# Row tiles that take every fourth row: a GeGLU feed-forward kernel on one Trainium2 core

## The chip, the cores and the metric

The kernel runs on one core of one Trainium2 chip. The metric is device time in microseconds (us) of one execution. "Median" is that of several executions. One execution of each kernel also left a profile, and this is the trace that is read. The span in a profile is about 1.9 us shorter than the device time of the same execution (before: 540.66 us and 538.8 us).

## The reference

```python
B, S, Dm, Df = 1, 2048, 1024, 3584          # all arrays bf16
def reference(x, w_gate, w_up, w_down):
    g = einsum("bsd,df->bsf", x, w_gate)
    u = einsum("bsd,df->bsf", x, w_up)
    h = gelu_tanh(g) * u
    return einsum("bsf,fd->bsd", h, w_down)
```

## The kernel before

The kernel makes the two products with fewer multiplications by block sums (the tiles `t`, `s`, `q`) and keeps TensorE (PE) busy nearly all the time. It works in two passes of 1024 rows. Only the first 512 rows of x come in as plain row tiles, which PE transposes; later rows come through transposing DMAs. All DMAs are issued by SyncE (SP), in program order, so the weights of the first matmuls stand in the queue behind the four x tiles. The first 8 us or so, until the row of matmuls that is never broken again, are called the head below. A load "lands" when its last bytes are reported in place.

```python
P, N = 128, 512;  NS = N // P                # 4 row tiles in 512 rows; Dm = 1024, so a row of x is 2 KB

def load_x(c):                               # called once, with c = 0
    t = []
    for i in range(NS):
        xn = slot([P, Dm], bf16, "xn")
        r0 = c * N + i * P
        nc.sync.dma_start(out=xn, in_=x2[r0 : r0 + P, :])
        t.append(xn)
    return t

def turn(xT, xn, c, i):                      # 8 transposes on PE, then copies to xT
    ...
        nc.tensor.transpose(tp[:, ko, :], xn[i][:, ko * P : (ko + 1) * P], ident)
    ...

xT = new_x()
xn0 = load_x(0)
wf = wpool.tile([P, 2, NKB, 2 * P], bf16, name="w")
for k0, k1 in ((0, 2), (2, 5), (5, NKB)):    # six slices of the first weights, pieces of 512 B
    load_wf(nc.sync, k0, k1)
w = load_w(1)
for ko in range(NKB):
    transposing(xT, 1, ko, N)                # rows 512 to 1023
...
keep_warm(NWARM, N)                          # matmuls of a constant while x comes in
for i in range(NS):
    if i == 2:
        keep_warm(2, 2 * P)
    turn(xT, xn0, 0, i)
plain(bank[0:4], 0, range(0, 2), parts=2)    # the first real matmuls: xT against wf
...

def store(ip, c, i, dc, put):                # 128 rows x 512 columns of the output
    st = slot([P, N], bf16, "st")
    put(st)
    r0 = (2 * ip + c) * N + i * P
    nc.sync.dma_start(out=out2[r0 : r0 + P, dc * N : (dc + 1) * N], in_=st)
```

## Time and profile before

| | before |
|---|---|
| median of the first three runs | 539.89 us (539.87 to 540.21) |
| span of the profiled run | 538.8 us |
| PE busy | 534.1 us, 99% |
| first unbroken row of matmuls starts at | 7.91 us |
| fourth x tile: issue, landing | 2.12 us, 6.99 us |

These are lines of the page of the kernel before: its span, busy time by engine (busy us, share, instructions), and the chain that ended last by engine.

```profile
span 538.8 us, 7447 instructions
...
PE 534.1 (99%) x2409; PEld 381.2 (71%) x2409; DVE 341.5 (63%) x524; ACT 261.4 (49%) x463; POOL 238.5 (44%) x215
...
PE 98%; DMA 1%; SPq 0%; ACT 0%; issue 0%
```

PE is the limit, and there is next to nothing else in the chain. This is the chain that ended last, in order of time (start, length in us, what), of the kernel before:

```profile
2.12 4.87 DMA xn<-in_x_dram
6.99 0.05 issue
7.04 0.62 PE bank L447 x8
7.66 0.22 PE bank L111 x2
7.88 0.03 issue
7.91 527.77 PE bank L111 x2366
```

The chain starts with the wait for the last x tile, goes through its eight transposes, and then stays on PE without a break for 527.77 us.

The timeline of PE in the first microseconds, before (start, us, engine, line, operation; in brackets the idle time ahead of the group and what ended it):

```profile
3.71 1.71 PE L447 MATMUL bank<-ident,xn 128*128 128x128 bf16 x16
...
6.31 1.35 PE L447 MATMUL bank<-ident,xn 128*128 128x128 bf16 x16 [0.66 <-DMA xn<-in_x_dram]
7.49 1.68 PE L111 MATMUL bank<-xT,w 128*128 128x256 bf16 x12
```

And the tiles `xn` before: their issue, and the time from issue to landing over the four of them.

```profile
L440 SPq DMA_DIRECT2D xn<-in_x_dram x4: 392/420/432, 0.7 to 2.1; - x4
...
DMA to landing us min/median/max: 2.8/3.8/4.9
```

The first tile lands 2.8 us after its issue, the fourth 4.9 us after. What the DMA moved meanwhile is in the table by windows (last three columns: granted PE clock, DMA share, GB/s):

```profile
2.50:5.00 2.50, 2.50 (x17) 1.62 (x16) 0.19 (x1) 0.00 (x0) 0.00 (x0) 1.00 1.04 316
5.00:7.50 2.50, 1.73 (x25) 1.28 (x24) 1.04 (x2) 2.02 (x2) 0.00 (x0) 1.00 1.11 320
```

### The profile page before, as it was taken

The numbers are of one execution on the slowest core, as the hardware profiler recorded it, in microseconds if no ns is written. First come the engines' busy times: TensorE is split into PE (matmuls) and PEld (weight loads), VectorE is DVE, ScalarE is ACT, GpSimd is POOL, SyncE is SP. The second block draws the span as 40 slices with busy tenths as digits, with TensorE's granted clock in tenths as the row PEclk, the third lists the DMA queues.
The fourth block names the chain that finished last, engine by engine and source line by source line (L and its number), as shares of the span: only waits on it lengthen the run. The fifth ranks groups of instructions, "written<-read, shape, count | busy, mean of one in ns | idle before, by whom it ended". The sixth has DMA issues, their size and how long they took to land.

```text
span 538.8 us, 7447 instructions
## 1 busy us (share of the span) xinstructions
PE 534.1 (99%) x2409; PEld 381.2 (71%) x2409; DVE 341.5 (63%) x524; ACT 261.4 (49%) x463; POOL 238.5 (44%) x215
## 2 busy tenths in 40 slices
PE   8999999999999999999999999999999999999997
PEld 5568686867677746888867677676868685488886
DVE  2986766767676894694955455555554649676730
ACT  2556675766666410255355555555555551114431
POOL 1179966677773500000097767676766600000000
DMA  9675656749472999989872223242420049573751
GB/s 243 157 185 168 185 176 175 220 133 260 131 235 72 381 366 297 307 192 296 238 195 80 78 80 88 70 118 63 133 71 9 2 147 390 184 236 96 237 181 51
DMA packets 108198, 93.29 MB, mean 173 GB/s; under 512 B 17280, under 2 KB 93056, under 8 KB 108160
## 3 DMA queue, kind: packets, MB, share of 16 engines
q1 hardware_dynamic: 108160, 92.82, 59.4%
q8 instruction: 19, 0.31, 0.3%
q14 instruction: 19, 0.16, 0.1%
HBM read 74.45 MB, written 15.20 MB: 166 GB/s over the span
## 4 chain that ended last, share of the span: by engine, by line
PE 98%; DMA 1%; SPq 0%; ACT 0%; issue 0%
PE bank L111 98%; DMA xn<-in_x_dram 1%; SPq L440 0%; PE bank L447 0%; ACT st L412 0%
## 5 line engine op out<-in xcount | busy, mean ns | idle before, releaser
L93 POOL TENSOR_TENSOR s<-w 128x512 fp32r<-128x512 bf16 x102 | 119.2, 1189 | 163.2 <-DVE t L90 86.0
L111 PE MATMUL bank<-t,s 128*128 128x512 f32 x648 | 151.7, 390 | 0.0
L111 PEld LDWEIGHTS bank<-t,s 128*128 128x128 f32 x648 | 121.6, 188 | 25.5
L111 PE MATMUL bank<-xT,w 128*128 128x512 bf16 (+1 forms) x504 | 109.7, 376 | 0.0
L107 ACT COPY p<-bank 128x512 f32<-128x512 f32 x124 | 69.9, 590 | 45.4 <-PE bank L111 44.9
L111 PEld LDWEIGHTS <-w 128*128 128x128 bf16 x504 | 48.1, 98 | 58.1 <-issue 3.4
L90 DVE TENSOR_TENSOR hT<-g,bank 128x512 bf16<-128x512 f32 x112 | 76.8, 687 | 17.5 <-PE bank L111 4.5
L90 DVE TENSOR_TENSOR sum<-bank,p 128x512 f32<-128x512 f32 x54 | 37.3, 691 | 79.5 <-PE bank L111 78.4
L179 ACT ACTIVATE g<-sum 128x512 f32<-128x512 f32 x81 | 51.4, 635 | 74.5 <-DVE sum L90 74.2
L111 PE MATMUL bank<-q 128*128 128x512 f32 x240 | 58.9, 389 | 0.0
L93 POOL TENSOR_TENSOR s<-w,s 128x512 fp32r<-128x512 bf16 x50 | 57.7, 1176 | 0.0
L93 POOL TENSOR_TENSOR s<-s,w 128x512 fp32r<-128x512 f32 x50 | 57.2, 1165 | 0.0
L111 PE MATMUL bank<-t,sa 128*128 128x512 f32 x216 | 55.9, 401 | 0.0
L111 PE MATMUL bank<-tb,s 128*128 128x512 f32 x216 | 53.3, 389 | 0.0
L107 ACT COPY u<-bank 128x512 f32<-128x512 f32 x62 | 35.5, 589 | 33.5 <-PE bank L111 33.2
L111 PEld LDWEIGHTS bank<-q 128*128 128x128 f32 x240 | 45.0, 188 | 9.4
L111 PE MATMUL bank<-raw,hT 128*128 128x512 bf16 x224 | 48.7, 379 | 0.0
L102 ACT CAST tb<-raw 128x512 fp32r<-128x512 bf16 x28 | 17.3, 626 | 62.1 <-PE bank L111 27.6
L111 PEld LDWEIGHTS bank<-t,sa 128*128 128x128 f32 x216 | 40.6, 188 | 9.5
L111 PEld LDWEIGHTS bank<-tb,s 128*128 128x128 f32 x216 | 40.5, 188 | 8.4
L90 DVE TENSOR_TENSOR bank<-bank,p 128x512 f32<-128x512 f32 x54 | 37.7, 699 | 8.8 <-PE bank L111 6.2
L90 DVE TENSOR_TENSOR q<-hT 128x512 fp32r<-128x512 bf16 x56 | 38.4, 685 | 4.3 <-PE bank L111 4.3
(44 smaller groups left out, 442.1 us busy)
## 6 DMA issues: line engine op xcount, KB each, us to landing
raw<-in_w_down_dram SPq DMA_DIRECT2D x76, 256.0 KB, 5.0
q<-td SPq DMA_DIRECT2D x60, 256.0 KB, 5.1
w<-in_w_gate_dram SPq DMA_DIRECT2D x27, 512.0 KB, 5.9
w<-in_w_up_dram SPq DMA_DIRECT2D x27, 512.0 KB, 7.0
td<-m SPq DMA_DIRECT2D x12, 768.0 KB, 4.5
w<-td SPq DMA_DIRECT2D x6, 1024.0 KB, 10.0
out_dram<-st SPq DMA_DIRECT2D x32, 128.0 KB, 1.7
td<-w SPq DMA_DIRECT2D x2, 768.0 KB, 6.2
```

The costliest lines, as they stand in the source:

```text
L90: nc.vector.tensor_tensor(out=out, in0=a, in1=b, op=op)
L93: nc.gpsimd.tensor_tensor(out=out, in0=a, in1=b, op=op)
L102: nc.scalar.copy(out=t, in_=src)
L107: nc.scalar.copy(out=t, in_=ps)
L111: nc.tensor.matmul(ps, lhsT=lhs, rhs=rhs, start=start, stop=stop, skip_group_check=True)
L179: nc.scalar.activation(g, src, ACT.Gelu_apprx_tanh)
```

## The change

The four row tiles of the first 512 rows are dealt out differently: tile i takes rows i, i+4, i+8 and so on. Each tile is still 128 pieces of 2 KB, but they start 8 KB apart (this distance is called the pitch below), and a tile spans 1 MB of memory and not 256 KB. The matmuls see the same rows in another order. The outputs of those rows come out in that order too, so their eight stores (of 32) write to every fourth row. The change gives no reason; a different layout in memory, of these reads and of eight stores, is all that it can act on.

```diff
 def store(ip, c, i, dc, put):
     ...
-    r0 = (2 * ip + c) * N + i * P
-    nc.sync.dma_start(out=out2[r0 : r0 + P, dc * N : (dc + 1) * N], in_=st)
+    r0 = (2 * ip + c) * N
+    rows = slice(i, N, NS) if ip == c == 0 else slice(r0 + i * P, r0 + i * P + P)
+    nc.sync.dma_start(out=out2[rows, dc * N : (dc + 1) * N], in_=st)

 def load_x(c):
     ...
-        r0 = c * N + i * P
-        nc.sync.dma_start(out=xn, in_=x2[r0 : r0 + P, :])
+        nc.sync.dma_start(out=xn, in_=x2[c * N + i : (c + 1) * N : NS, :])
```

No engine gains or loses an instruction, and their order stays the same on every engine.

## The prediction

> **What bounds the kernel.** TensorE. The page's first table gives PE 534.1 us of a 538.8 us span (99%); the chain of waits is 98% matmuls of one line, unbroken from 7.91 to 535.7 us. The part of the chain that is not PE is the head: 4.87 us in which the fourth x tile is awaited (issued at 2.12 us, landed at 6.99), then eight transposes, then the first matmuls, which wait another 0.31 us for the first w_up slice. By the timeline PE idles about 1.6 us from its first warm-up matmul to 8 us, so little more can be won there.
>
> **What the change does.** Four loads of 256 KB (x, first 512 rows) and eight of the 32 stores (128 KB each) keep their count, bytes and pieces: 128 rows of 2 KB in, 128 rows of 1 KB out. Only the pitch in HBM changes, from 2 KB to 8 KB between row starts, so each tile spans the whole first 1 MB instead of a quarter. Every engine's instructions stand in the same order. The transposed columns hold other rows, and the stores undo it. No compute is removed or added.
>
> **Cost.**
> - Loads. In the first 8 us the DMA moves 310 to 370 GB/s in most half-microsecond windows, so the head is limited by x (1 MB, an estimate of 3 us at that rate) and the weights queued behind it. The tiles land 2.8, about 3, 4.6 and 4.9 us after issue; the third is late beside one straggling packet of 1.5 us (median 84 ns). The pitch may move stragglers by a fraction of a microsecond. A check for pitch: q from the td scratch, 256 KB in 2 KB rows at 84 KB pitch, lands in 5.1 us median, w_down tiles of 256 KB in 5.0 us. So I expect no slower rate. The Trainium skill (DMA: Bandwidth & Descriptors, Latency and other measured facts, "HBM row pitch at large powers of two") tabulates row pitches from 512 KiB up, slower from 2 MiB on; 8 KiB is far below, and no run here yet shows it. Effect: 0, give or take 0.7 us, one for one in the total.
> - Stores. Their landing (1.7 us median) is awaited once by DVE (1.1 us, at 264 us, for a buffer of the t sums); those sums are done by 273 us and PE takes them at 279 us. Even a doubled landing stays off the chain. Effect: 0.
>
> **Prediction.** 539.8 us, 8 in 10 between 538.7 and 541.0. Chance of faster by over 2%: 0.005; within 2%: 0.985; slower by over 2%: 0.01.
>
> **Right or wrong in the profile.** Right: PE busy 534 us within 0.5, the chain still 98% matmuls, x loads landing in 2.8 to 5 us, the unbroken matmuls starting within 0.7 us of before, stores landing in 1.7 to 2.5 us, DVE's wait for a store under 3 us. Any change of the total equals the shift of that start (7.91 us before). Wrong: x landing after 8 us, or a new PE gap later.
>
> **What would make it wrong.** A pitch of 8 KB that piles the engines' reads onto fewer parts of HBM: x would land at half rate and the head lose an estimated 3 us, still 0.6%. Or reads of one contiguous 256 KB are the ones that collide (the straggler), and spreading them brings the head forward by up to 1.3 us. Or a late store holds a buffer that PE needs soon: a new gap near 215 or 265 us.

## The result, and the profile after

| | before | after |
|---|---|---|
| median, 6 runs each | 540.01 us (539.84 to 540.21) | 541.78 us (541.11 to 542.14) |
| ratio | | 1.0031 (95%: 1.0018 to 1.0044) |
| span of the profiled run | 538.8 us | 540.1 us |
| unbroken matmuls start at | 7.91 us | 9.02 us |

Ratios here and below are the mean time of one kernel's runs over that of the other's runs of the same rounds, so they are not quite the ratio of the medians quoted. The change costs 1.8 us here, 0.3%: well under 2%, but clear of the spread. The whole range of after lies above 541.0 us, the top of the predicted range.

The page after:

```profile
span 540.1 us, 7447 instructions
...
PE 534.6 (99%) x2409; PEld 381.0 (71%) x2409; DVE 341.5 (63%) x524; ACT 261.2 (48%) x463; POOL 237.8 (44%) x215
...
PE 98%; DMA 1%; SPq 0%; ACT 0%; issue 0%
```

The chain that ended last, after:

```profile
2.12 5.93 DMA xn<-in_x_dram
8.05 0.05 issue
8.10 0.62 PE bank L447 x8
8.72 0.25 PE bank L111 x2
8.97 0.05 issue
9.02 527.96 PE bank L111 x2366
```

The work is the same. The fourth x tile takes 5.93 us and not 4.87 us, and the unbroken matmuls start 1.11 us later. That is most of the 1.3 us between the two spans; the row of matmuls itself took 0.19 us more in this trace. The timeline of PE after shows new gaps, each ended by an x tile:

```profile
4.23 1.78 PE L447 MATMUL bank<-ident,xn 128*128 128x128 bf16 x16 [0.31 <-DMA xn<-in_x_dram]
...
6.57 0.62 PE L447 MATMUL bank<-ident,xn 128*128 128x128 bf16 x8 [0.34 <-DMA xn<-in_x_dram]
8.10 0.62 PE L447 MATMUL bank<-ident,xn 128*128 128x128 bf16 x8 [0.91 <-DMA xn<-in_x_dram]
8.58 0.39 PE L111 MATMUL bank<-xT,w 128*128 128x256 bf16 x2
```

All x tiles land later, while their issues take as long as before:

```profile
L440 SPq DMA_DIRECT2D xn<-in_x_dram x4: 392/418/432, 0.7 to 2.1; - x4
...
DMA to landing us min/median/max: 3.4/4.4/5.9
```

The windows after show the same loss as a rate: the same queue of loads moves 238 and 262 GB/s in place of 316 and 320. The DMA share (time of packets over the time of 16 engines; it passes 1 where packets overlap) falls with it, from 1.04 and 1.11 to 0.77 and 0.95. By the packet records the median x packet took 84 ns in both traces. So most of the loss is time with fewer packets under way, and not slower packets.

```profile
2.50:5.00 2.50, 2.19 (x12) 1.00 (x10) 0.00 (x0) 0.00 (x0) 0.00 (x0) 1.00 0.77 238
5.00:7.50 2.50, 1.85 (x21) 1.17 (x18) 0.97 (x2) 1.44 (x2) 0.00 (x0) 1.00 0.95 262
```

The first weight slices moved with x: they landed 4.8 us after their issue before, and 5.9 us after it now. The Trainium skill ("DMA: Bandwidth & Descriptors", "Queues, rings and completion order") says that each DMA engine consumes its descriptors in ring order. The landings agree with that: what stands behind x slips by the same 1.1 us.

What opens the unbroken row is a load of weights into PE (PEld), and it waits for the first slice of `w_up`, the second load behind x. First before, then after (timeline of PEld, window 2:10):

```profile
7.91 2.07 PEld L111 LDWEIGHTS <-w 128*128 128x128 bf16 x18 [0.31 <-DMA w<-in_w_up_dram]
...
9.01 0.99 PEld L111 LDWEIGHTS <-w 128*128 128x128 bf16 x10 [0.32 <-DMA w<-in_w_up_dram]
```

That slice landed at 7.87 us before and at 8.97 us after. In all eleven kernel traces with four x tiles and these slices behind them (before, after, e1, e2, e6 to e10, f2, f3) this weight load starts 0.04 to 0.05 us after that landing. So the chain's first step, the wait for x, is not quite the last wait: x and the slice behind it slip together, and the slice releases the row.

### The profile page after: what moved, and what is told of

The parts are those of the page before. It is cut to its first block, busy times and chain, and to the rows that moved or that the text cites. A ratio compares the mean times of both kernels' runs of the same rounds, so it can differ in the third digit from the quotient of the medians.

```text
span 540.1 us, 7447 instructions
## 1 busy us (share of the span) xinstructions
PE 534.6 (99%) x2409; PEld 381.0 (71%) x2409; DVE 341.5 (63%) x524; ACT 261.2 (48%) x463; POOL 237.8 (44%) x215
## 4 chain that ended last, share of the span: by engine, by line
PE 98%; DMA 1%; SPq 0%; ACT 0%; issue 0%
PE bank L111 98%; DMA xn<-in_x_dram 1%; SPq L440 0%; PE bank L447 0%; ACT st L413 0%
```

## The experiments

**Theory H**: the loss is in the head. At a pitch of 8 KB the x loads run slower, and PE's first matmuls wait for them and for the weights behind them. **Rival S**: the eight stores are slower, and hold buffers that something needs. **Rival N**: the one trace of each is luck. (The trace before has a straggler, an x packet of 1.5 us where the median is 84 ns; it is not a lucky trace.)

Inside H it was open whether any break of the sequence is slow, or a pitch that is a power of two, or 8 KB alone, and whether other traffic has a part in it.

The table gathers what ran as a whole kernel. "Before" is the kernel before in the same rounds; each of the four batches of rounds (e1 and e2; e6 to e8; e9 to e12; f2 and f3) ran on another chip. Landing is that of the fourth x tile after its issue, in the one trace of each.

| run | what | median | before | ratio (95%) | landing |
|---|---|---|---|---|---|
| e1 | strided loads alone | 541.34 us | 540.26 us | 1.0018 (1.0005 to 1.0030) | 5.2 us |
| e2 | strided stores alone | 540.27 us | 540.26 us | 0.9997 (0.9983 to 1.0010) | 4.2 us |
| e8 | the change again | 541.29 us | 540.22 us | 1.0023 (1.0009 to 1.0037) | 5.4 us |
| e6 | every second row | 540.42 us | 540.22 us | 1.0006 (0.9994 to 1.0019) | 5.0 us |
| f2 | every third row | 540.33 us | 540.19 us | 1.0003 (0.9991 to 1.0016) | 4.4 us |
| f3 | every eighth row | 540.33 us | 540.19 us | 1.0008 (0.9994 to 1.0022) | 4.3 us |
| e7 | rows dealt, 32 apart | 540.66 us | 540.22 us | 1.0012 (1.0000 to 1.0025) | 4.3 us |
| e9 | weights held back, rows as before | 543.48 us | 540.26 us | 1.0061 (1.0049 to 1.0074) | 4.2 us |
| e10 | weights held back, every fourth row | 544.63 us | 540.26 us | 1.0084 (1.0070 to 1.0098) | 4.4 us |
| e11 | pieces of 4 KB | 540.84 us | 540.26 us | 1.0022 (1.0008 to 1.0035) | |
| e12 | one load, pieces of 8 KB | 542.56 us | 540.26 us | 1.0040 (1.0026 to 1.0053) | |

### e1 and e2: one half of the change each

```diff
 e1: load_x as after, store as before      (output wrong on purpose: its rows are permuted)
 e2: load_x as before, store as after      (likewise)
```

> The first 512 rows are loaded with the new pitch, but their outputs are stored in sequence as before, so the output is wrong on purpose. Theory H (the loss sits in the head: the four x loads run slower at a pitch of 8 KB): the whole loss appears, 1.3 to 2.2 us over before, with the fourth x tile landing about 5.5 to 6.2 us after its issue. Rival S (the stores, or the buffers they hold, cost it): within 0.4 us of before.

> The loads are as before and only the eight stores go to every fourth row, so the output is wrong on purpose. Theory H: within 0.3 us of before. Rival S: 1.3 to 2.2 us over before.

The loads alone cost 1.1 us, the stores alone nothing. The chains that ended last say where, first of e1 and then of e2:

```profile
3.07 5.39 DMA w<-in_w_up_dram
8.46 0.05 issue
8.51 527.75 PE bank L111 x2366
```

```profile
2.12 4.17 DMA xn<-in_x_dram
6.29 0.05 issue
6.34 0.62 PE bank L448 x8
6.96 0.38 PE bank L111 x2
7.33 0.03 issue
7.37 527.76 PE bank L111 x2366
```

The rows of matmuls are equally long (527.75 and 527.76 us), and start 1.14 us apart. In e1 the chain's head is the first `w_up` slice and not x: the slice that releases the row in e2 too. Rival S falls. The loss in e1 (1.1 us) is at the low end of what was expected or under it (1.3 to 2.2 us), and its fourth tile landed at 5.2 us, not 5.5 to 6.2. The repeat, e8, gives the same 1.1 us for the whole change; the 1.8 us of the first rounds was not met again.

> The changed kernel itself, timed on the same chip as the others. Theory H: 1.0 to 1.9 us over before, the first unbroken matmuls later by the same amount as in the earlier trace, about 1.1 us or more.

In e8's trace the unbroken matmuls start at 8.54 us. Against the first trace before (7.91 us) that is only 0.63 us later, less than the 1.1 us expected; against e2's, whose loads are the same as before (7.37 us), it is 1.17 us. The trace before has the straggler, so e2's is the better base.

### e3 and e4: the loads by themselves

A kernel with nothing but loads: four x tiles issued one after the other, the next group when all four have landed; twelve groups of each kind, in rotating order.

```diff
+for name, rows in order:                     # row steps 1, 2, 3, 4, 5, 8, 16; in e4 four layouts
+    for i, t in enumerate(tiles):
+        nc.sync.dma_start(out=t, in_=rows(i))
+    for t in reversed(tiles):                # the next group waits for these reads
+        nc.vector.tensor_copy(out=acc[:, 0:64], in_=t[:, 0:64])
```

> Only loads, output wrong on purpose: groups of four 256 KB tiles of x in 2 KB rows, each group started when the one before has landed, twelve times each at row steps 1, 2, 3, 4, 5, 8 and 16 (2 to 32 KB pitch), in rotating order. Time from a group's first issue to its last landing. Theory H: step 4 takes 0.8 to 2 us longer than step 1. Within H: if a power-of-two pitch piles reads on fewer parts of memory, steps 4, 8 and 16 are slow and 3 and 5 as fast as 1, the loss growing with the step; if what counts is that neighbouring rows are no longer read together, steps 2 to 16 are all slow alike. Rival N (not the pitch but the unlucky start of a run): all steps within 0.3 us.

Median landing after issue, twelve groups each, in us:

| row step (pitch) | 1 (2 KB) | 2 (4) | 3 (6) | 4 (8) | 5 (10) | 8 (16) | 16 (32) |
|---|---|---|---|---|---|---|---|
| first tile | 2.6 | 2.6 | 2.6 | 3.2 | 2.7 | 3.0 | 2.7 |
| fourth tile | 4.0 | 3.8 | 4.2 | 4.3 | 4.1 | 3.8 | 3.9 |

(With steps 2 and 3, here and in e5, some of the four tiles read the same rows again, so the steps from 4 on are the cleaner comparison.) Step 4 is the slowest, but by only 0.3 us, at the fourth tile and from a group's first issue to its last landing (5.60 against 5.32 us), which is not the 0.8 to 2 us that theory H expected. The loss does not grow with the pitch. So H has the right place, but loads of x by themselves do not explain 1.1 us.

> Only loads, output wrong on purpose: groups of four tiles as in the other load kernel, in four layouts: rows in sequence; every fourth row; runs of four rows in sequence (8 KB) with a gap of 12 rows between runs, so that a tile spans 1 MB; and rows of one contiguous 256 KB dealt to the partitions with a step of 32 rows between neighbouring partitions. If what counts is that four neighbouring rows go to neighbouring partitions, the runs are as fast as the sequence and the dealt rows as slow as every fourth row. If what counts is the span of 1 MB or the common pitch between tiles, the runs are slow and the dealt rows fast. Differences wanted: 0.8 us or more of about 4 to 6 us.

The first tile landed at 2.7 us in sequence, 3.1 us at step 4, 3.0 us for runs of four rows, and 2.9 us for dealt rows; the fourth tile at 4.0, 4.3, 4.1 and 3.7 us. None of the wanted differences of 0.8 us is there: inconclusive about layout, but it points at what is missing, the work behind x.

### e5 and f1: loads with other loads behind them

```diff
 for i, t in enumerate(tiles):
     nc.sync.dma_start(out=t, in_=rows(i))
+if weights:                                  # the kernel's first six weight slices, 1 MB
+    for n, (k0, k1) in enumerate(((0, 2), (2, 5), (5, 8))):
+        for src in (w_gate, w_up):
+            nc.sync.dma_start(out=..., in_=src[k0 * P : k1 * P, 0:256].rearrange(...))
```

> Only loads, output wrong on purpose: groups of four x tiles in sequence or at every fourth row, alone and with the kernel's first six weight slices (1 MB in pieces of 512 B) queued behind them, and with the weights also at row steps 2, 3, 16 and in the layout dealt with a step of 32 rows. Theory A (the weights queued behind widen the loss: an engine done with its x rows starts on weights and slows the ones that still read x): the fourth tile lands 0.3 us later at step 4 when alone, and 0.8 to 1.3 us later with the weights behind. Rival C (the weights play no part; it is the cold start of a launch): 0.3 us later in both.

These are the fourth tiles of e5: in sequence and at step 4 alone, then both with the weights behind (tile names one_d, four_d, onew_d, fourw_d). The second line of each pair is the time to landing over twelve groups.

```profile
L40 SPq DMA_DIRECT2D one_d<-in_x_dram x12: 430/430/432, 2.1 to 970.7; - x12
...
DMA to landing us min/median/max: 3.8/4.1/4.4
...
L40 SPq DMA_DIRECT2D four_d<-in_x_dram x12: 381/382/432, 8.8 to 977.1; - x12
...
DMA to landing us min/median/max: 4.0/4.2/4.7
...
L40 SPq DMA_DIRECT2D onew_d<-in_x_dram x12: 376/430/430, 15.5 to 983.7; - x12
...
DMA to landing us min/median/max: 3.6/4.1/4.6
...
L40 SPq DMA_DIRECT2D fourw_d<-in_x_dram x12: 424/430/430, 26.2 to 912.8; - x12
...
DMA to landing us min/median/max: 4.7/5.5/6.4
```

In sequence, the weights behind x cost x nothing (4.1 and 4.1 us). At step 4 they turn 4.2 us into 5.5 us. So a difference of 0.1 us alone becomes 1.4 us with other loads queued behind, although these were issued after x; 0.3 us and 0.8 to 1.3 us were expected. The twelve groups of each do not even overlap: the least at step 4 (4.7 us) is above the largest in sequence (4.6 us). So rival N falls, and so does rival C, a cold start as the cause. With the weights behind, steps 2, 3 and 16 had their fourth tile at 4.5, 4.5 and 4.6 us, and dealt rows at 4.1 us: again only step 4 stands out.

> Only loads, output wrong on purpose: groups as in the earlier load kernels. With the six weight slices behind: row steps 1, 4, 6, 8. With 1 MB of w_down in full rows (pieces of 2 KB) behind: steps 1 and 4. With weights read as pieces of 512 B in sequence behind: steps 1 and 4. Step 4 over step 1 at the fourth tile was 1.4 us with the weights. If the small pieces are what slows x, the difference with w_down behind falls to 0.5 us or less and stays above 1 us with small pieces in sequence; if any traffic behind will do, it is above 1 us in all three; if it is the weights' own pitch of 7 KB, only with the weights. Pitch 8 KB in particular: steps 6 and 8 within 0.7 us of step 1.

Median landing of the fourth tile in f1, in us:

| behind x | step 1 | step 4 | step 6 | step 8 |
|---|---|---|---|---|
| the weight slices (512 B pieces, 7 KB apart) | 4.4 | 5.8 | 4.7 | 4.6 |
| 1 MB of w_down in sequence (2 KB pieces) | 4.5 | 6.0 | | |
| weights in sequence (512 B pieces) | 4.4 | 5.5 | | |

Any of the three will do: the loss is 1.4, 1.5 and 1.1 us, so it needs neither the small pieces nor their pitch. And 12 KB and 16 KB pitch are within 0.3 us of the sequence.

### e6, f2, f3: other pitches in the kernel itself

```diff
 e6:  in_=x2[r0 : r0 + 2 * P - 1 : 2, :]  with r0 = i // 2 * 2 * P + i % 2; stores likewise, output right
 f2:  in_=x2[i : i + 3 * (P - 1) + 1 : 3, :]      stores as before, output wrong on purpose
 f3:  in_=x2[i : i + 8 * (P - 1) + 1 : 8, :]      likewise
```

> Every second row of 256 instead of every fourth of 512 (a pitch of 4 KB), the stores likewise, output right. If any break of the sequence costs the head, 0.8 to 1.8 us over before. If it is the pitch of 8 KB in particular, as the load kernel says (fourth tile 3.8 us at step 2, 4.0 in sequence, 4.3 at step 4), within 0.4 us of before.

> The kernel before with the first x tiles read at every third row (a pitch of 6 KB), stores as before, so the output is wrong on purpose. The load kernel with weights behind had the fourth tile 0.4 us and the last weights 0.2 us later than in sequence: 0.1 to 0.6 us over before. If any gap between rows costs as much as every fourth row: 1.0 us or more.

> The kernel before with the first x tiles read at every eighth row (a pitch of 16 KB), output wrong on purpose. If the loss grows with power-of-two pitches: 1.5 us or more over before. If 8 KB stands out: 0.2 to 0.8 us over before.

Pitches of 4, 6 and 16 KB came out 0.2, 0.1 and 0.1 us over before by medians, each interval holding 1. (In f2 the fourth tile reads almost the rows of the first again.) Their intervals and e8's overlap in part; only e6 shares e8's rounds, and its five times (540.02 to 540.85 us) all lie under e8's (541.25 to 541.68 us). That 16 KB is better than 8 KB rests on the load kernels more than on f3. In e6's trace the fourth tile was late all the same (5.0 us); one trace of a load is one draw. The result is "8 KB in particular", as the load kernels had said; f3 and f2 fall at or just under the low ends of what was expected. So neither the permutation of rows as such nor leaving the sequence is enough to explain 1.1 us.

### e9 and e10: the weights held back

```diff
 xn0 = load_x(0)
+hold = dpool.tile([1, Dm], bf16, name="hold")
+nc.sync.dma_start(out=hold, in_=xn0[3][:1])     # waits for the fourth tile; the weights come after it
```

> The kernel before, with the weights held back: a copy of one row of the fourth x tile to a scratch stands ahead of them in the queue, so they are issued only when that tile has landed. Output right. The weights land later, so the time should rise by an estimated 2.5 to 4 us over before. It is the base for the next run: fourth tile expected about 4.0 us after issue.

> The changed kernel with the weights held back in the same way. Output right. Theory A (the loss needs the weights behind x): fourth tile at about 4.3 us, and the time within 0.6 us of the held-back kernel before. Rival C (the weights play no part): 1.0 to 1.9 us over it, the fourth tile about 1 us later than there.

With nothing behind x, the fourth tile lands 4.2 us after issue in sequence (first fence, e9) and 4.4 us at step 4 (second fence, e10): the difference of 1.0 us or more has gone from the landing of x in the kernel too.

```profile
L440 SPq DMA_DIRECT2D xn<-in_x_dram x1: 432/432/432, 2.1 to 2.1; - x1
...
DMA to landing us min/median/max: 4.2/4.2/4.2
```

```profile
L440 SPq DMA_DIRECT2D xn<-in_x_dram x1: 432/432/432, 2.1 to 2.1; - x1
...
DMA to landing us min/median/max: 4.4/4.4/4.4
```

The times do not follow. Holding back alone cost 3.2 us, as expected, but the two medians, 543.48 us (five runs) and 544.63 us (four runs), are still 1.15 us apart, where 0.6 us at most was expected. Holding the weights back delays all that stands behind them as well, and the chain of e10 runs through that: the issue of the transposing loads and the landing of the last one, up to PE's start at 27.14 us. It is no longer the wait for x at the head, and e9's chain does not go that way. In these two traces the first `w_up` slice, with x already in, landed at 9.42 us in e9 and at 10.09 us in e10, and the row began 0.67 us apart; one trace of each does not tell whether that is chance.

```profile
24.40 2.70 DMA xT<-in_x_dram
27.10 0.04 issue
27.14 8.97 PE bank L111 x39
```

So this pair supports the part of the weights by the landing of x alone; as a test of the total it failed, and why e10 is slower there is not settled.

### e7, e11, e12: is there a better way to deal the rows?

```diff
 e7:   dealt = x2[0:N, :].rearrange("(i b a) d -> i a b d", i=NS, b=4);  in_=dealt[i]   (stores likewise)
 e11:  two loads, rows 4p and 4p+1, then 4p+2 and 4p+3, to partition p: pieces of 4 KB
 e12:  one load, rows 4p to 4p+3 to partition p: pieces of 8 KB
```

e11 and e12 keep the stores of the change and land in a part of hT that is idle then. The output of all three is right.

> Each tile reads its own 128 rows in sequence in memory, but neighbouring partitions take rows 32 apart (a pitch of 64 KB), the stores likewise, output right. The load kernel had its fourth tile at 3.7 us against 4.0 in sequence: up to 0.5 us under before if that carries over, and within 0.4 us in any case. If neighbouring rows in neighbouring partitions are what counts: 0.8 to 1.8 us over before.

> The changed rows, but read as two transfers of 512 KB in which a partition takes two neighbouring rows as one piece of 4 KB, into a buffer that is idle then. Output right. Two issues fewer put the weights about 0.9 us earlier in the queue. If the number of pieces and issues sets the head: 0.3 to 0.9 us under before. If a pitch of 8 KB alone is slow: 0.3 to 1.5 us over before.

> The changed rows in one transfer of 1 MB, a partition taking four rows as one piece of 8 KB, so that memory is read in sequence again. Output right. Landing about 4.5 us after 0.74 us, but all four transposes come behind it (4 times 0.65 us): within 0.7 us of before. The weights are issued 1.4 us earlier.

None beats the kernel before. In e7 the fourth tile lands 4.3 us after issue, no sooner than in e2 (4.2 us), so the gain of the load kernel did not carry over; each load now has a pattern of one dimension more and takes 0.58 to 0.68 us to issue in place of 0.39 to 0.43, so that the fourth is issued at 2.74 us and not at 2.12. It came out 0.44 us over before by medians, just outside the 0.4 us allowed. In e11 the first two tiles come together and 1 MB lands no sooner: the second pair is transposed from 6.64 us, against 6.31 us for the third and fourth tile in the trace before; it was 0.6 us over before, not under. In e12 all four tiles are transposed behind one landing at about 5.7 us, and the first matmul comes at 9.52 us: 2.3 us over before, far more than the 0.7 us allowed.

## Why the prediction was wrong

- **The step that failed** is the term for the loads: "So I expect no slower rate ... Effect: 0, give or take 0.7 us, one for one in the total." It measured 1.1 us in e1 and e8, and 1.8 us in the first rounds (541.78 against 540.01 us). "One for one" was right: the matmuls started 1.11 us later in the trace, where "within 0.7 us" had been named as the sign of being right. The prediction knew that the first matmuls also wait for the first w_up slice; it is this slice, queued behind x and landing 5.9 us after issue in place of 4.8, that releases the row.
- **The check behind it was no check.** The `q` loads (pitch of 84 KB, 5.1 us) against w_down loads (5.0 us) say nothing of 8 KB: the load kernels show that 4, 6, 16 and 32 KB stay within 0.5 us of the sequence at the fourth tile, alone or with loads behind; 8 KB does so only alone. A comparison at one other pitch cannot clear this one.
- **The skill's figure was read for more than it says.** "DMA: Bandwidth & Descriptors", section "Latency and other measured facts", "HBM row pitch at large powers of two", tabulates pitches from 512 KiB up. That a smaller one must be harmless was mine. The runs differ: 8 KB costs 1.1 to 1.5 us at the fourth tile once other loads are behind. Nor does the loss grow with the pitch: 16 KB is better than 8 KB.
- **The named danger had the right direction.** "A pitch of 8 KB that piles the engines' reads onto fewer parts of HBM: x would land at half rate and the head lose an estimated 3 us" was given as what might go wrong. The rate fell by about a fifth and a quarter (320 to 262, and 316 to 238 GB/s) and not by half. That the reads are piled on fewer parts of memory is not shown by any run here.
- **The straggler was not the change's to win.** In the trace of e2, whose loads are in sequence, the fourth tile landed 4.2 us after issue and the matmuls began at 7.37 us, and yet the median did not move (540.27 against 540.26 us). That is a hint that the usual run before has no straggler so late. The trace before is of an execution of 540.66 us, 0.65 us over the median of the six timed ones, about what its row of matmuls started later than e2's (0.54 us). So the change's loss looks smaller between the two first traces (1.3 us) than between the medians (1.8 us).
- **Right:** PE is the limit (534.6 us busy after, 534.1 before), the chain stays 98% matmuls, the stores cost nothing (e2: ratio 0.9997), and no new PE gap came later. The one wait of DVE for a store went from 1.1 to 0.3 us.
- **A small misreading:** stores were said to land in 1.7 to 2.5 us. The median of all 32 is 1.7 us. The first four land in 4.4 to 5.5 us before and 4.9 to 6.4 us after, among other loads; in the trace of e2 it is 5.0 to 6.4 us. Nothing waits for these four.

What stays open: why 8 KB, of all pitches tried, is slow, and how loads queued behind can slow x ahead of them. The records of packets do not say which DMA engine moved which, so this can be read from these traces only in part. They hold sixteen landing reports for each load, of which `prof` prints the last. In e3, with x alone, the sixteen reports of a group's first tile span 1.15 us at step 4, against 0.38 us in sequence and 0.49 to 0.96 us at the other steps (medians of twelve groups): at 8 KB some of the sixteen shares of a load come late from the start. In e5 the span at the fourth tile is 0.79 us at step 4 alone and 1.95 us with the weights behind (in sequence 0.98 and 1.14 us). That fits theory A, that whatever is early goes on to the loads behind while the late shares stay late, but it does not prove it. Nor is it settled why the held-back pair is 1.15 us apart in time.

## What to carry to other kernels

Look at the head of a kernel as a stage of its own: at 99% busy PE, the wait for the first data still counts one for one, and the bytes and pieces of a load do not tell its time. Measure a new access pattern with the traffic that will stand behind it, since here a difference of 0.1 us alone was 1.4 us in company. If rows must be dealt out for another reason, try a pitch beside the one in question: 4, 6 and 16 KB cost 0.2 us or less by the medians where 8 KB cost 1.1 us.

## What the Trainium skill lacked or had wrong

- "DMA: Bandwidth & Descriptors", "HBM row pitch at large powers of two", starts at 512 KiB. A row pitch of 8 KB with pieces of 2 KB is slow as well: fourth tile at 5.5 us against 4.1 us in sequence, once other loads stand behind it (e5), while 16 KB (4.6 against 4.4 us in f1) and 32 KB (4.6 against 4.1 us in e5) lose less.
- The same page does not say that such a loss can depend on what is queued behind: 4.2 against 4.1 us alone, 5.5 against 4.1 us in company (e5), whatever the size of the pieces behind (f1).
- The same page gives no issue time by number of dimensions: in the kernels here a load of 256 KB took 0.39 to 0.43 us to issue with one row step, and 0.58 to 0.68 us with a row pattern of two steps (e7).
